# Copies, evictions and Abs on either of two engines, shorter product steps, fillers on TensorE and later stores of x in a planned retention + two-MoE kernel

## The chip, the cores and the metric

One core of a Trainium2 chip. The metric is device time in microseconds, from one launch; the kernel before has a median of 885.75 us over three runs (883.87 to 886.39).

## The reference, cut to what matters

Retention (attention without softmax, with a decay mask) over 4 batches, 8 heads, 576 positions of 64, then two dense feed-forward layers of 512 to 2048 to 512 on 2304 tokens.

```python
scores = q @ k.T / 8
x = (scores * Dmat) @ v             # Dmat[i, j] = gamma[h] ** (i - j) for i >= j, else 0
h = x @ moe_w_in
x = (h * cos(h)) @ moe_w_out
h = x @ moe2_w_in
out = (maximum(h, 0) + log1p(exp(-abs(h)))) @ moe2_w_out
```

## The kernel before, in words

**Number format.** Each fp32 operand of the two MoE layers is split in a high part (fp32r, made by a copy on ScalarE) and a low part (the difference, made by `sub`, L270, on VectorE or GpSimd). A product is three matmuls: high by high, high by low, low by high.

**A plan orders everything.** The kernel is written as some 3,500 steps (`op`): an engine, a cost in us, a key (when the step is wanted, in the plan's own clock), a function that issues the instructions, and tokens read and written. `Plan.order` runs a list schedule: of the steps whose inputs are there, the one that can start first goes next, and among equals the one with the lower key. Each engine's instruction stream is then issued in that order, and an engine works through its stream in order. A step of the kind "pool or dve" is put on GpSimd or VectorE, whichever gives the lower start + FLEX x cost. `port` keeps GpSimd and the VectorE steps marked with `port=True` apart in the plan. DMAs (`dma`, L262) all go out from SyncE's queue and never before key - LEAD (7.381) in the plan. `t_mm`, `t_act`, `t_dve`, `t_dve2`, `t_pool` are the costs. Tiles come from rings: a new tile waits for all users of the one whose place it takes.

**Attention.** 32 pieces (`piece`, L652 on: `front`, `masks`, `states`, `back`, `after`), each one pair of heads and half a sequence: fp32 scores on TensorE (L529), masks on VectorE, the state sums (L534, L584, L588), values and carried parts (L606), then the high and low part of x (L641, L270). The first 16 pieces run alone; the other 16 lie between the steps of the first MoE groups (`SPREAD`). Before the first piece three warm-up matmuls of 350 zero columns run (L900). `raw` is the tile that a piece's q, k, v load fills (ring of 5).

**Layer 1, part A** (`moe_a`, `slot`, `mm_in` L693, `out1` L789): five groups of tokens (512, 512, 384, 384, 512), the first 8 of 16 blocks of the hidden width. `x_store(m)` writes a group's x (xdh, xdl) to device memory for the rest of the layer. The partial sums are copied out of PSUM (`ev`, L935) and stored as pd. Weights come as 64-bit-viewed words and are put together from bits (`convert`: L317 and L323 on ScalarE, L329, L336 or L332, L336, L340 on VectorE; then wh, L363, and wl, L270).

**The rest** (`moe_c`, `quad`) is three phases of five token blocks by four pairs of hidden blocks: the second half of layer 1 and the two halves of layer 2. A quad of 512 tokens makes seven products of half-size blocks instead of eight (a Strassen-like scheme): product 1 into R1, 2 into R2, 5 into R3; copy_1 (L847) and copy_5 (L851) save R1 and R3; one step then does products 6 (on R1) and 3 (on R3); copy_6 (L854) saves R1; L860 adds both copies to R2 and R3; product 7 goes onto R1, L863 makes R4 from R1 and the saved R3, and product 4 ends R1. Product matmuls have the line L823, 256 columns each, six to a product. `activate` is the nonlinearity: layer 1 scales to turns (L729), takes the remainder (L733), Abs (L736), Sin (L739) and the product (L742); layer 2 uses L753, Softplus (L756) and L759. Then gh (L768, ScalarE) and gl (L270, VectorE) feed the output matmuls (L884, up to 512 columns). Results are added to what was stored (L1105) or, in the first phase of layer 2, copied out of PSUM (`ev`, L1095). While a phase runs, `weight_pair` makes the next pairs of weights (L394, L415, L423) and `x_load_c` the next block of x (L1013, L1020).

The plan's clock has marks: M[m], when group m of part A begins, and MB, when the quads begin (`M0` plus the groups' costs). Before the change M0 = 27.414.

Of the kernel before, what the change touches and what calls it, by code (L numbers as in the profile page):

```python
# [32 lines left out]
def t_mm(n, m=128):  # L33
    return max(n / 2236.0 + 0.001, 0.107 * m / 128)
# [24 lines left out]
POOL_DVE = "pool or dve"  # L59

# [6 lines left out]
FLEX = 0.364  # L67
# [33 lines left out]
class Plan:  # L101
# [29 lines left out]
    def order(self):  # L131
# [32 lines left out]
        for _ in range(n):  # L164
            best = None
            for i in can:
                eng, dur, key, _, _, uses_port, _ = self.ops[i]
                if eng == POOL_DVE:
# [10 lines left out]
            t, _, i, dur, eng = best  # L179
            can.remove(i)  # L180
# [14 lines left out]
            if uses_port or what == POOL_DVE:  # L195
                port = t + dur
# [27 lines left out]
def retention_moe_moe(ctx, tc, qkv, w1, w2, mask, mtail, dq, dk, out):  # L224
# [128 lines left out]
    def weight(layer, f, key, step):  # L353
        wk = ("w", layer, f)
        for z in range(2):
# [16 lines left out]
            op(POOL_DVE, 512, k + 2.8, lo, r=[ak, th], w=[tl])  # L372
# [284 lines left out]
    def piece(firsts, seconds, backs, K):  # L657
# [13 lines left out]
        op("pe", sum(p["dur"] for p in ps) + 0.35, K, run, r=[t for p in ps for t in p["r"]],  # L671
# [48 lines left out]
    def activate(layer, e, h_k, n, i, K1):  # L720
# [5 lines left out]
        if layer == 1:  # L726
# [8 lines left out]
            def a4():  # L735
                nc.scalar.activation(e["r"], e["r"], AF.Abs)  # L736
# [9 lines left out]
            op("act", t_act(n), K1 + 1.4, a4, r=[r_k], w=[r_k])  # L746
# [51 lines left out]
    def quad(layer, q, xk, n, K, u, acc_id, acc, first, last):  # L798
# [40 lines left out]
        if n == 512:  # L839
# [5 lines left out]
            def copy_1():  # L845
                e["cv"] = wp["q"].tile([128, 512], F32, tag="cv", name="cv", bufs=2)
                nc.scalar.activation(e["cv"][:, 0:256], R1(), AF.Copy)  # L847

            def copy_5():
                e["c5"] = wp["q"].tile([128, 256], F32, tag="c5", name="c5", bufs=2)  # L850
                nc.scalar.activation(e["c5"], R3(), AF.Copy)  # L851

            def copy_6():
                nc.scalar.activation(e["cv"][:, 256:512], R1(), AF.Copy)  # L854
# [334 lines left out]
```

## Time and profile before

| | |
|---|---|
| median of three runs | 885.75 us |
| the profiled run's own time | 888.67 us |
| its span, first to last instruction | 886.9 us |
| TensorE busy | 860.3 us (97%) |
| VectorE busy | 606.1 us (68%) |
| ScalarE busy | 488.5 us (55%) |
| GpSimd busy | 134.8 us (15%) |
| mean granted TensorE clock | 0.994 |

A matmul's busy time includes the tail of the pipeline, so neighbours overlap and the busy share does not say how near the engine is to its peak; its idle time is real. The same holds for the durations of VectorE and ScalarE: the next instruction starts a little before the end of the one before. DVE is VectorE, ACT is ScalarE, PE is TensorE and PEld its weight load, POOL is GpSimd, SPq is SyncE's queue. `L823 <- ACT cv L847` reads: line 823 waited for what ScalarE wrote to cv on line 847.

### The profile page before, as it was taken

Reading aid. Unit: us, or ns where it says so; the run is one execution under the profiler, and the core shown is the slowest. Engines: PE = TensorE matmul, PEld = TensorE weight load, DVE = VectorE, ACT = ScalarE, POOL = GpSimd, SP = SyncE. Lnnn points to the kernel's source line nnn. Section 1 sums busy time; section 2 is a strip of 40 time slices with the busy share of each in tenths; the row PEclk is TensorE's granted clock in tenths of the full one; section 3 lists DMA queues with packets and bytes.
Section 4 is the critical chain, followed back from the end, with each engine's and each line's share of the span. In section 5 each row is a group of like instructions: output and inputs, shape, how many; then the busy total and the mean of one; then the engine's idle time right before and its main releaser. Section 6 shows DMA issues by size and latency. Waiting matters only on the chain.

```text
span 886.9 us, 15054 instructions
## 1 busy us (share of the span) xinstructions
PE 860.3 (97%) x5766; PEld 748.5 (84%) x5766; DVE 606.1 (68%) x1107; ACT 488.5 (55%) x984; POOL 134.8 (15%) x143
## 2 busy tenths in 40 slices
PE   8999999999999999999999999999999999999998
PEld 5766777899988888888888888898898989898887
DVE  3799744564499986567588997467559985464554
ACT  1477743545577865546777875355547863333322
POOL 3622000100031260022053341020001010000000
PEclk8999999999999999999999999999999999999999
DMA  9886323432325612226355628065453925241202
GB/s 317 347 322 225 123 81 131 165 133 92 119 99 163 229 49 95 87 86 191 107 209 180 197 75 308 17 257 204 141 215 122 351 104 195 114 148 72 95 31 77
DMA packets 56233, 139.14 MB, mean 157 GB/s; under 512 B 5088, under 2 KB 24672, under 8 KB 54112
## 3 DMA queue, kind: packets, MB, share of 16 engines
q1 hardware_dynamic: 56160, 138.18, 44.2%
q8 instruction: 45, 0.74, 0.3%
q14 instruction: 28, 0.23, 0.1%
HBM read 93.59 MB, written 44.56 MB: 156 GB/s over the span
## 4 chain that ended last, share of the span: by engine, by line
PE 73%; DVE 9%; DMA 7%; ACT 5%; issue 3%; SPq 1%; POOL 1%; DVEq 0%; POOLq 0%; ACTq 0%
PE acc L884 26%; PE acc L789 10%; PE o L823 7%; PE hb L823 7%; PE ha L823 5%; PE s L823 5%; PE hb L693 4%; PE ha L693 3%; DMA wr<-in_w 2%; PE o L606 1%; SPq L262 1%; DVE wk L329 1%; PE s L693 1%; PE o L693 1%; DVE gl L270 1%
## 5 line engine op out<-in xcount | busy, mean ns | idle before, releaser
L884 PE MATMUL acc<-pair,gh 128*128 128x512 f32 x576 | 180.1, 393 | 0.0
L884 PE MATMUL acc<-pair,gl 128*128 128x512 f32 x288 | 113.6, 394 | 0.0
L884 PEld LDWEIGHTS acc<-pair,gh 128*128 128x128 f32 x576 | 99.4, 188 | 14.9 <-ACT gh L768 0.4
L884 PE MATMUL acc<-gh,pair 128*128 128x512 f32 (+1 forms) x320 | 103.4, 375 | 2.2 <-DVE pt L1105 1.4
L756 ACT ACTIVATE er<-er 128x512 f32<-128x512 f32 (+1 forms) x80 | 47.1, 589 | 76.3 <-DVE er L753 76.2
L823 PE MATMUL o<-x,pair 128*128 128x256 f32 x328 | 78.0, 282 | 2.5 <-ACT cv L847 2.3
L823 PE MATMUL o<-xx,pair 128*128 128x256 f32 x320 | 77.5, 284 | 2.0 <-DVE o L863 1.4
L823 PE MATMUL hb<-x,pair 128*128 128x256 f32 x328 | 77.9, 281 | 1.4 <-DVE hb L863 0.8
L823 PE MATMUL hb<-xx,pair 128*128 128x256 f32 x320 | 77.0, 282 | 1.0 <-DVE hb L863 1.0
L884 PEld LDWEIGHTS acc<-gh,pair 128*128 128x128 f32 x320 | 59.5, 192 | 11.2 <-DVE pt L1105 1.6
L884 PEld LDWEIGHTS acc<-pair,gl 128*128 128x128 f32 x288 | 54.0, 188 | 13.2 <-DVE gl L270 0.5
L884 PE MATMUL acc<-gl,pair 128*128 128x512 f32 (+1 forms) x160 | 60.8, 380 | 3.5 <-DVE gl L270 3.5
L736 ACT ACTIVATE er<-er 128x512 f32<-128x512 f32 (+2 forms) x80 | 46.9, 586 | 31.3 <-DVE er L733 30.1
L823 PEld LDWEIGHTS o<-x,pair 128*128 128x128 f32 x328 | 57.6, 188 | 7.6 <-ACT cv L847 2.9
L823 PEld LDWEIGHTS hb<-x,pair 128*128 128x128 f32 x328 | 57.6, 188 | 6.6 <-DVE hb L863 1.5
L823 PEld LDWEIGHTS o<-xx,pair 128*128 128x128 f32 x320 | 56.3, 188 | 7.6 <-DVE o L863 3.1
L823 PEld LDWEIGHTS hb<-xx,pair 128*128 128x128 f32 x320 | 56.3, 188 | 5.8 <-DVE hb L863 2.0
L789 PE MATMUL acc<-gh,wh 128*128 128x512 f32 (+1 forms) x160 | 60.2, 376 | 0.5 <-ACT gh L768 0.5
L789 PE MATMUL acc<-gl,wh 128*128 128x512 f32 (+1 forms) x160 | 59.4, 372 | 0.8 <-DVE gl L270 0.7
L789 PE MATMUL acc<-gh,wl 128*128 128x512 f32 (+1 forms) x160 | 58.9, 368 | 0.0
L823 PE MATMUL s<-x,pair 128*128 128x256 f32 x256 | 58.3, 280 | 0.0
L823 PE MATMUL ha<-x,pair 128*128 128x256 f32 x256 | 58.2, 279 | 0.0
(197 smaller groups left out, 2073.2 us busy)
## 6 DMA issues: line engine op xcount, KB each, us to landing
wr<-in_w SPq DMA_DIRECT2D x64, 512.0 KB, 4.0
raw<-in_qkv SPq DMA_DIRECT2D x12, 640.0 KB, 7.2
raw<-in_qkv SPq DMA_DIRECT2D x12, 512.0 KB, 5.7
od<-pt SPq DMA_DIRECT2D x18, 256.0 KB, 3.9
pt<-od SPq DMA_DIRECT2D x18, 256.0 KB, 2.8
out<-pt SPq DMA_DIRECT2D x18, 256.0 KB, 2.1
pt<-pd SPq DMA_DIRECT2D x16, 256.0 KB, 3.1
yd<-pt SPq DMA_DIRECT2D x16, 256.0 KB, 2.1
```

The lines of the kernel that those rows point to most:

```text
L262: nc.sync.dma_start(dst(), src())
L270: e.tensor_tensor(out_, a, hi.bitcast(F32), ALU.subtract)
L329: nc.vector.scalar_tensor_tensor(T["wk", u], T["wy", u], 3, T["wr", u][:, :, 0], ALU.logical_shift_left, ALU.bitwise_or)
L606: nc.tensor.matmul(o_at(z)[Z[j]], lhs(j), rhs(j), start=start, stop=stop, skip_group_check=True)
L693: nc.tensor.matmul(h_[:, 0:n], lhs, rhs[:, d, 0:n], start=(k == 0), stop=(k == 3 * NC - 1))
L736: nc.scalar.activation(e["r"], e["r"], AF.Abs)
L756: nc.scalar.activation(e["r"], e["r"], AF.Softplus)
L789: nc.tensor.matmul(acc[o][:, 0:n], l[:, s], e[r], start=(first and z == 0), stop=(last and z == 2))
L823: nc.tensor.matmul(out_, w_(a), x_(b), start=(start and y == 0), stop=(stop and y == 5), skip_group_check=True)
L884: nc.tensor.matmul(acc[m][:, 0:n] if layer == 1 else acc[m], l, r, start=(begin and z == 0), stop=(stop and z == 2))
```

## The change

Five things: (1) a new kind of step, "act or dve", for the three copies of a quad, the two kinds of eviction (`ev`) and Abs of layer 1 (on VectorE Abs is a bitwise and with 0x7FFFFFFF); (2) products 6 and 3 become two steps with keys of their own, and copies and adds of a quad get keys EARLY or EARLY_2 lower; (3) after pieces 0 and 1 two and five matmuls of 128 zero columns; (4) x_store's key goes from M + 30 to M + 60; (5) other constants of the plan. AHEAD is empty, so its loop in `order` does nothing, and LO_A keeps its step as it was.

```diff
-def t_mm(n, m=128):
-    return max(n / 2236.0 + 0.001, 0.107 * m / 128)
+def t_mm(n):
+    return n / 2236.0 + (0.0035 if n == 256 else 0.001)
...
+ACT_DVE = "act or dve"
...
-FLEX = 0.364
+FLEX = 0.27
+FLEX_AD = 0.824
...
-W2 = (16.989, 6.589, 8.458, 3.942)
-W3 = (16.475, 1.639)
-XC = 4.126
-LAG_C = 1.17
+W2 = (18.111, 6.589, 14.31, 1.214)
+W3 = (16.671, 1.958)
+XC = 3.809
+LAG_C = 1.049
 TT = 3
+TURN = 0.6
+XS = 60.0
+FILL = (2, 5)
+EARLY = 12.734
+EARLY_2 = 8.236
...
-LL = 1.121
+LL = 0.916
...
-W0 = (34.558, 4.019, 3.451)
-M0 = 27.414
+W0 = (39.65, 2.003, 3.451)
+M0 = 28.787
 AK = (1.0, 2.2)
-PAIR_A = 0.566
+PAIR_A = 0.959
...
+                elif eng == ACT_DVE:
+                    t, d, e = min(
+                        ((max(ready[i], free[e], port if e == "dve" and uses_port else 0.0), d, e) for e, d in zip(("act", "dve"), dur)),
+                        key=lambda o: o[0] + FLEX_AD * o[1])
...
-            if uses_port or what == POOL_DVE:
+            if uses_port and eng != "act" or what == POOL_DVE:
                 port = t + dur
...
+    def copy(eng, out_, in_):
+        if eng is nc.scalar:
+            nc.scalar.activation(out_, in_, AF.Copy)
+        else:
+            eng.tensor_copy(out_, in_)
...
-        op("pe", sum(p["dur"] for p in ps) + 0.35, K, run, r=[t for p in ps for t in p["r"]],
+        op("pe", sum(p["dur"] for p in ps) + TURN, K, run, r=[t for p in ps for t in p["r"]],
...
-            dma(lambda g=g: xd[g][:, :, r0:r0 + n], lambda g=g: T[xk][g][:, :, 0:n].bitcast(F32), 512 * n * 4, M[m] + 30 + g, r=XT[m], w=[("xd", g, m)])
+            dma(lambda g=g: xd[g][:, :, r0:r0 + n], lambda g=g: T[xk][g][:, :, 0:n].bitcast(F32), 512 * n * 4, M[m] + XS + g, r=XT[m], w=[("xd", g, m)])
...
-            def a4():
-                nc.scalar.activation(e["r"], e["r"], AF.Abs)
+            def a4(eng):
+                if eng is nc.scalar:
+                    nc.scalar.activation(e["r"], e["r"], AF.Abs)
+                else:
+                    r = e["r"].bitcast(I32)
+                    nc.vector.tensor_scalar(r, r, 0x7FFFFFFF, None, ALU.bitwise_and)
...
-            op("act", t_act(n), K1 + 1.4, a4, r=[r_k], w=[r_k])
+            op(ACT_DVE, (t_act(n), t_dve2(n)), K1 + 1.4, a4, r=[r_k], w=[r_k], port=True)
...
-            op("act", t_act(256, True), K + 0.7, copy_1, r=[r1, ("qopen",)], w=[(ck, 0)], new=[("cv", 2, ck)])
-            op("act", t_act(256, True), K + 2.1, copy_5, r=[r3, ("qopen",)], w=[(c5k,)], new=[("c5", 2, c5k)])
-            pe([P(R1, 6, False), P(R3, 3, False)], K + 1.0, [r1, r3])
-            op("act", t_act(256, True), K + 4.0, copy_6, r=[r1], w=[(ck, 1)])
-            op("dve", t_dve(512), K + 4.5, lambda: nc.vector.tensor_tensor(ea["h"], ea["h"], e["cv"], ALU.add),
+            op(ACT_DVE, (t_act(256, True), t_dve(256)), K + 0.7 - EARLY, copy_1, r=[r1, ("qopen",)], w=[(ck, 0)], new=[("cv", 2, ck)])
+            op(ACT_DVE, (t_act(256, True), t_dve(256)), K + 2.1 - EARLY, copy_5, r=[r3, ("qopen",)], w=[(c5k,)], new=[("c5", 2, c5k)])
+            pe([P(R1, 6, False)], K + 0.9, [r1])
+            pe([P(R3, 3, False)], K + 1.5, [r3])
+            op(ACT_DVE, (t_act(256, True), t_dve(256)), K + 4.0 - EARLY, copy_6, r=[r1], w=[(ck, 1)])
+            op("dve", t_dve(512), K + 4.5 - EARLY_2, lambda: nc.vector.tensor_tensor(ea["h"], ea["h"], e["cv"], ALU.add),
                r=[(ck, 0), (ck, 1)], w=[r2, r3])
             pe([P(R1, 7, False)], K + 2.0, [r1])
-            op("dve", t_dve(256), K + 5.5, lambda: nc.vector.tensor_tensor(R4(), R1(), e["c5"], ALU.add), r=[r1, (c5k,)], w=[r4])
+            op("dve", t_dve(256), K + 5.5 - EARLY, lambda: nc.vector.tensor_tensor(R4(), R1(), e["c5"], ALU.add), r=[r1, (c5k,)], w=[r4])
...
+    def fill(n, times):
+        for _ in range(times):
+            nc.tensor.matmul(T["warm", "o"][:, 0:n], T["warm"][:, 0:128], T["warm"][:, 0:n], start=True, stop=True)
...
-            op("act", t_act(n, True), K, ev, r=[(ak,)], w=[pk], new=[("pt", PT, pk[0])])
+            op(ACT_DVE, (t_act(n, True), t_dve(n)), K, ev, r=[(ak,)], w=[pk], new=[("pt", PT, pk[0])])
...
+        if i < len(FILL) and FILL[i]:
+            op("pe", FILL[i] * t_mm32(128), AK[0] + AK[1] * i + 0.1, lambda i=i: fill(128, FILL[i]), r=[U[i]["x"][0], (("er", "warm"),)],
+               w=[(("hb", "warm"),)])
...
-                op("act", t_act(DM, True), K, ev, r=[(ak,)], w=[(pk,)], new=[("pt", PT, pk)])
+                op(ACT_DVE, (t_act(DM, True), t_dve(DM)), K, ev, r=[(ak,)], w=[(pk,)], new=[("pt", PT, pk)])
```

## Rows read from the trace of the kernel before

**Rows 1.** Busy us by stretch; each engine's (x instructions), then PEclk, DMA share, GB/s.

```profile
0.00:9.00 9.00, 5.75 (x30) 3.35 (x30) 1.30 (x4) 1.51 (x2) 2.24 (x9) 1.00 0.74 229
9.00:15.82 6.82, 6.28 (x60) 4.87 (x60) 2.96 (x9) 1.06 (x4) 2.85 (x6) 0.50 1.02 355
15.82:45.00 29.18, 28.55 (x488) 22.17 (x488) 22.12 (x79) 10.79 (x33) 16.91 (x26) 1.00 0.92 360
45.00:100.00 55.00, 50.14 (x350) 38.10 (x346) 50.85 (x99) 41.30 (x82) 10.79 (x14) 1.00 0.75 260
...
281.00:345.00 64.00, 59.88 (x369) 52.11 (x368) 56.30 (x92) 46.83 (x91) 21.01 (x16) 1.00 0.45 149
345.00:380.00 35.00, 35.00 (x212) 30.74 (x211) 18.96 (x32) 19.50 (x38) 1.73 (x2) 1.00 0.24 76
380.00:420.00 40.00, 36.62 (x268) 34.06 (x267) 28.21 (x54) 21.12 (x49) 8.39 (x6) 0.96 0.43 136
...
440.00:532.00 92.00, 88.06 (x540) 76.78 (x540) 80.24 (x125) 70.58 (x139) 36.04 (x33) 1.00 0.48 161
...
600.00:620.00 20.00, 18.36 (x120) 16.21 (x119) 15.61 (x26) 11.45 (x24) 1.68 (x1) 1.00 0.53 204
620.00:886.90 266.90, 262.68 (x1632) 234.78 (x1630) 168.65 (x284) 118.32 (x236) 9.50 (x12) 1.00 0.38 140
sum 886.90, PE 860.30 PEld 748.55 DVE 606.13 ACT 488.54 POOL 134.83; mean PE 66.18 PEld 57.58 DVE 46.63 ACT 37.58 POOL 10.37
```

**Rows 2.** Waits of TensorE: line and what it waited for, total us, times, longest.

```profile
PE acc L884 <- DVE gl L270: 3.5, 7, 1.4
PE o L823 <- ACT cv L847: 2.9, 3, 1.3
...
PE ha L693 <- ACT wh L363: 1.9, 1, 1.9
PE s L529 <- DVE st L588: 1.8, 1, 1.8
PE hb L823 <- DVE hb L863: 1.8, 2, 1.0
...
PE o L823 <- DVE o L863: 1.4, 1, 1.4
```

**Rows 3.** Busy us in the second half-clock stretch, columns as in rows 1.

```profile
391.29:394.70 3.41, 3.41 (x14) 3.18 (x15) 1.18 (x4) 1.18 (x4) 0.00 (x0) 0.50 0.15 43
```

**Rows 4.** TensorE in order of time, start: us, start, duration, [idle before <- releaser].

```profile
1.45 3.87 PE L900 MATMUL hb<-er 128*128 128x350 f32 x6 [1.45 <-DVE er L895]
...
6.83 0.71 PE L529 MATMUL acc<-raw 64*128 64x128 f32 x8 [0.73 <-DMA raw<-in_qkv]
...
9.54 1.23 PE L529 MATMUL acc<-raw 64*128 64x128 f32 x8 [1.61 <-DMA raw<-in_qkv]
...
18.17 0.72 PE L529 MATMUL acc<-raw 64*128 64x128 f32 x8
```

**Rows 5.** SyncE's queue in order of time, the first store of x.

```profile
55.03 0.58 SPq L262 DMA_DIRECT2D xdh<-x  x1
```

**Rows 6.** ScalarE in order of time, before the wait for wh.

```profile
73.58 0.67 ACT L323 ACTIVATE wr<-wr 128x512 int32<-128x512 uint8 x1 [2.14 <-DMA wr<-in_w]
```

**Rows 7.** ScalarE in order of time, ahead of a late copy_1.

```profile
454.88 0.63 ACT L736 ACTIVATE er<-er 128x512 f32<-128x512 f32 x1 [1.24 <-DVE er L733]
455.42 0.62 ACT L1020 ACTIVATE xx<-tt 128x512 fp32r<-128x512 f32 x1
...
457.03 0.37 ACT L847 ACTIVATE cv<-o 128x256 f32<-128x256 f32 x1
```

**Rows 8.** VectorE in order of time, the two adds of a quad.

```profile
530.06 0.69 DVE L860 TENSOR_TENSOR s<-s,cv 128x512 f32<-128x512 f32 x1
530.66 0.42 DVE L863 TENSOR_TENSOR o<-o,c 128x256 f32<-128x256 f32 x1
```

**Rows 9.** Line 332: duration in ns (min/median/max), first and last start in us, forms.

```profile
L332 DVE TENSOR_SCALAR wk<-wy x16: 413/420/1506, 180.6 to 317.4; 128x512 int32<-128x512 int32 x16
```

More of the change, by code (lines that the diff above doesn't have):

```diff
@@ L74 @@
 WB = (21.627, 3.294)
-W2 = (16.989, 6.589, 8.458, 3.942)
-W3 = (16.475, 1.639)
-XC = 4.126
-LAG_C = 1.17
+W2 = (18.111, 6.589, 14.31, 1.214)
+W3 = (16.671, 1.958)
+XC = 3.809
+LAG_C = 1.049
 TT = 3
+TURN = 0.6
[3 more added lines that the diff above has]
+EARLY_2 = 8.236
+AHEAD = {}
+GAP = 2.0
+LO_A = "pool or dve"
 END = 3.1
 LC = 2.5
-LL = 1.121
+LL = 0.916
 LB = 1.9
@@ L179, in order @@
             t, _, i, dur, eng = best
+            if eng in AHEAD and dur > AHEAD[eng]:
+                for j in can:
+                    e, d, key = self.ops[j][:3]
+                    if j != i and e == eng and key < self.ops[i][2] - GAP and ready[j] < t + AHEAD[eng]:
+                        f = max(free[eng], ready[j], port if self.ops[j][5] else 0.0)
+                        if f < t + AHEAD[eng] and (f, key) < (t + AHEAD[eng], best[1]):
+                            best, t, i, dur = (f, key), f, j, d
             can.remove(i)
@@ L214, in emit @@
     def emit(self, nc):
-        flexible = {"pool": nc.gpsimd, "dve": nc.vector}
+        flexible = {"pool": nc.gpsimd, "dve": nc.vector, "act": nc.scalar}
         for i in self.order():
-            if self.ops[i][0] == POOL_DVE:
+            if self.ops[i][0] in (POOL_DVE, ACT_DVE):
                 self.ops[i][3](flexible[self.eng[i]])
@@ L371, in weight @@
                new=[(f"w{f}", 1, wk)] if z == 0 else [])
-            op(POOL_DVE, 512, k + 2.8, lo, r=[ak, th], w=[tl])
+            if LO_A == POOL_DVE:
+                op(POOL_DVE, 512, k + 2.8, lo, r=[ak, th], w=[tl])
+            else:
+                op("pool", t_pool(512), k + 2.8, lambda lo=lo: lo(nc.gpsimd), r=[ak, th], w=[tl], port=True)
     def weight_pair(layer, q, key, step):
@@ L843, in quad, with copy_1, copy_5, copy_6 @@
             e = {}
[L845 removed]
+            def copy_1(eng):
                 e["cv"] = wp["q"].tile([128, 512], F32, tag="cv", name="cv", bufs=2)
[L847 to L849 removed]
+                copy(eng, e["cv"][:, 0:256], R1())
+            def copy_5(eng):
                 e["c5"] = wp["q"].tile([128, 256], F32, tag="c5", name="c5", bufs=2)
[L851 to L860 removed]
+                copy(eng, e["c5"], R3())
+            def copy_6(eng):
+                copy(eng, e["cv"][:, 256:512], R1())
+            op(ACT_DVE, (t_act(256, True), t_dve(256)), K + 0.7 - EARLY, copy_1, r=[r1, ("qopen",)], w=[(ck, 0)], new=[("cv", 2, ck)])
[4 more added lines that the diff above has]
+            op("dve", t_dve(512), K + 4.5 - EARLY_2, lambda: nc.vector.tensor_tensor(ea["h"], ea["h"], e["cv"], ALU.add),
                r=[(ck, 0), (ck, 1)], w=[r2, r3])
             pe([P(R1, 7, False)], K + 2.0, [r1])
[L863 removed]
+            op("dve", t_dve(256), K + 5.5 - EARLY, lambda: nc.vector.tensor_tensor(R4(), R1(), e["c5"], ALU.add), r=[r1, (c5k,)], w=[r4])
             pe([P(R1, 4, False)], K + 3.0, [r1])
@@ L897, in warm @@
     def warm():
-        o_ = bank("hb")
-        for _ in range(3):
-            nc.tensor.matmul(o_[:, 0:WARM], T["warm"][:, 0:128], T["warm"][:, 0:WARM], start=True, stop=True)
+        T["warm", "o"] = bank("hb")
+        fill(WARM, 3)
+    def fill(n, times):
+        for _ in range(times):
+            nc.tensor.matmul(T["warm", "o"][:, 0:n], T["warm"][:, 0:128], T["warm"][:, 0:n], start=True, stop=True)
     if WARM:
```

9 lines of the change are left out of this document (5 added, 4 removed).

## The prediction

> **What bounds the kernel now.** I read the table of stretches first [rows 1]. TensorE is busy 860.30 of 886.90 us, so only 26.6 us are idle, and the table says where: 3.25 us before 9.00, 0.54 and 0.63 in the next two stretches, 4.86 from 45 to 100, 4.12 from 281 to 345, 3.38 from 380 to 420, 3.94 from 440 to 532, 1.64 from 600 to 620, 4.22 after 620 (nearly all the drain of the last store). The long stretches left out have 0.02. So this is a TensorE kernel with holes. The reader should see what the holes have in common: from 281 to 345 VectorE is busy 56.30 of 64 us (88%), from 440 to 532 80.24 of 92 (87%), and ScalarE 73% and 77%; from 345 to 380 VectorE is at 54% and TensorE loses nothing. The holes sit where weight conversion crowds the two elementwise engines.
>
> Second, TensorE's waits [rows 2]. The product steps (L823) wait 2.9 us for the copy L847 and 1.8 and 1.4 us for the add L863: 6.1 us in six waits. The output steps (L884) wait 3.5 us for gl (L270). In the first 100 us there are a 1.8 us wait for st and a 1.9 us wait for wh.
>
> Third, the clock. From 9.00 to 15.82 it is granted at 0.50, which is 1.2 GHz [rows 1], and again from 391.29 to 394.70 [rows 3].
>
> **The change, part by part.**
>
> *Fillers.* Two zero matmuls follow piece 0, five follow piece 1. Before the clock falls, TensorE stands 0.73 us ahead of piece 1 and 1.61 ahead of piece 2, both times for a load of raw; the eight score matmuls of a piece then take 1.23 us at half clock and 0.72 at full clock [rows 4]. The nearest price of a filler is the warm-up: six records, three matmuls of 350 columns, 3.87 us, so at most 0.47 us for 128 columns, and half of that at full clock. Seven cost 1.6 to 3.3 us against 2.34 us of standing; at the price nearest to theirs (the clock is full there) they fit, at the other end up to 1 us spills over. What they can give: 6.28 busy us at half clock hold 3.1 us of work that full clock would not need. But in that stretch the DMA engines are 1.02 busy at 355 GB/s and stay at 0.92 until 45, so faster pieces soon run into their loads. I take 2.0 us, from -1 to 3.1. The Trainium skill (TensorE: Matmul & The Clock Gate, Terms) puts the loss at throttled time times (1 - K/N); for both half-clock stretches together that is 5.1 us as an estimate, where busy time gives 4.8 and the loads, which that rule leaves out, leave less.
>
> *Later stores of x.* x_store moves from M+30 to M+60 in key: five pairs of issues on SP's queue move behind weight and qkv loads. The first pair is issued at 55.03 [rows 5], among the loads for the first MoE slots, when the DMA engines are 0.75 busy; ScalarE then stands 2.14 us for a weight load before L323 [rows 6], and the weight behind it ends in the 1.9 us wait for wh. W0's new keys (step 2.003 for 4.019) also bring later weights forward. Of the 4.86 us from 45 to 100 I take 2.5, from 0 to 4.9. What the move holds up: the store of group 2 frees the pool of the pair weights. By the constants M[2]+60-7.4 is 179 and the first pair's key M[3]+18.1 is 184, against the start of the quads at MB = 244, so this hides. The store of group 4 falls at M[4]+60-7.4 = 252, after MB, and tile x1 that it holds is wanted by the quads of the second block, whose turn is four quads of UC, 42 us, after MB. That hides too.
>
> *Copies of the quads (copy_1, copy_5, copy_6) and their adds.* They get keys 12.7 (the 512-wide add 8.2) earlier and may go to either engine. See one case: copy_1 stood in ScalarE's queue behind L736, L1020 and more, none of which the product step was waiting for; it waited until it ran at 457.03 [rows 7]. On VectorE the add L863 stood behind L860 from 530.06 to 530.66 and TensorE waited for it [rows 8]. With an early key a copy that is ready goes next, so what remains of a wait is the rest of the instruction in work, about 0.3 us (half of 0.6). Six waits of 6.1 us become 1.8: I take 4.5, from 0 to 6.1. On VectorE a copy from PSUM should cost about what L863 does, 0.42 us, against 0.37 for L847 on ScalarE [rows 7, 8]: either engine will do.
>
> *Shorter product steps.* Products 6 and 3 become two steps, so copy_6 may start after six matmuls instead of twelve and product 3 fills TensorE meanwhile. It adds no instruction. It pays in the few small waits on L854, below the rows shown, so I take 0.5, from 0 to 1.
>
> *Abs and evictions on either engine.* Abs costs 0.63 us on ScalarE [rows 7]. The nearest row on VectorE, a one-source integer operation of the same tile, has a median of 0.42 and a longest of 1.51 [rows 9]. This, with the copies leaving ScalarE's queue, shortens the chain to gl; but the copies now also jump ahead of gl on VectorE. Of gl's 3.5 us I take 2, from -3 to 3.5.
>
> *Clock at 391.* Half clock over 3.41 us costs 1.7; it follows TensorE's waits there. With shorter waits it may not fall: 1.0, from 0 to 1.7.
>
> *VectorE's extra load.* Whatever moves to it in the crowded stretches delays conversion: minus 1, from 0 to minus 4.4 (second rival). *The other constants* (t_mm, TURN, FLEX, M0, LL and the rest) only shift keys and the planner's clock. They add no instruction; what they reorder is hidden by the quiet stretches [rows 1], and where it isn't, it belongs to the terms above.
>
> Sum: 2.0 + 2.5 + 4.5 + 0.5 + 2 + 1 - 1 = 11.5 us. The profiled run took 888.67 us for a span of 886.9, 2.9 above the median of 885.75; I subtract from the median: 885.75 - 11.5 = 874.25, say **874.3**. With all upper ends (20.3) it would be 865.5; with the lower ends (-8.4) 894.
>
> **Rivals.** *The waits change hands.* The order on each engine is fixed in advance, so a copy that goes first makes gl or gh late: copies gain 4.5, gl loses 3, Abs and clock give nothing, start and x stores give 1: 885.75 - 2.5 = 883.2. For it: gl is already the longest wait [rows 2]. Against: a late copy holds up a whole quad, a late gl only one output group, behind which products can run.
>
> *VectorE becomes the bound.* In the three crowded stretches from 281 to 532 (196 us) VectorE has 31.3 us free [rows 1]. About 18 quads of 10.9 us pass in them (an estimate: a quad's 66 matmuls at the pace of 345 to 380, 212 in 35 us); three copies and two Abs on VectorE at 0.42 us less some 0.07 of overlap between neighbours (L863 starts 0.60 us after an L860 of 0.69) bring 5 x 0.35 = 1.75 us to each, 31.5 us in all, and fill it. From 54% to 88% busy the idle share of TensorE rose from 0 to 6.4%; on the same slope the last 12% cost 2.3% of 196 us, 4.4 us, and the gains of copies and gl go. 885.75 - 2 (start) + 4.4 = 888.2. It decides if more than about two thirds of the moved operations land on VectorE there. Against: the planner takes whichever engine starts and ends first, and ScalarE is the freer one. A rule of the Trainium skill speaks for this rival: GPSIMD Engine Reference, Specifications, says that GpSimd shares its SBUF interfaces with VectorE and contends with instructions in a two-port mode, which Abs on VectorE would be; rows 9 agree, with 1.51 us for what mostly takes 0.42.
>
> *The plan hardly uses it.* ScalarE stays first choice, the order stays nearly as it was, and only the start gains: 885.75 - 1.5 = 884.3.
>
> **How the numbers follow.** Forecast 0.69 (its own range 866 to 882), waits change hands 0.12, VectorE the bound 0.13, hardly used 0.06. About 0.3% (2.7 us, so 883.1) is what a measurement of this kernel can tell from no change. Faster: 0.69 and half of 0.12, 0.75. Same: the other half and the 0.06, 0.12. Slower: 0.13. The range is 864 to 887: it takes in the upper ends, both rivals near no change, and leaves out about 0.04 below and 0.11 above.
>
> **What would show it.** Fillers: granted clock 1.00 from 9 to 16, and the first MoE matmul about 2 us earlier. Stores: xdh first issued after 75, and no 1.9 us wait for wh. Copies: L823's waits for L847 and L863 sum to under 2 us. Abs: L736 on both engines. If VectorE goes over 93% busy in 281 to 345 and TensorE idles more there than 4.12 us, the second rival is right. If gl's waits pass 6 us, the first is. The prediction is wrong if the first 100 us or the quads keep their idle time.

## The result: 0.8% slower

The changed kernel has a median of **892.77 us** over five runs (891.21 to 895.03) beside 885.75 us for the kernel before (883.87 to 888.51) on the same chip: a ratio of 1.0082, interval 1.0055 to 1.011. The forecast of 874.3 us was wrong in its sign. The profiled runs lie closer together (892.48 against 888.67 us, spans 890.7 and 886.9), since the profile of before comes from a run 2.9 us above its median, and that of after from one 0.3 below. The changed kernel's busy times:

```profile
PE 861.9 (97%) x5780; PEld 751.2 (84%) x5780; DVE 633.0 (71%) x1169; ACT 454.2 (51%) x897; POOL 170.2 (19%) x168
```

Before it was 606.1 us and 1107 instructions on VectorE, 488.5 and 984 on ScalarE, 134.8 and 143 on GpSimd. ScalarE lost 87 instructions: the copies, evictions and Abs that went to VectorE. VectorE has only 62 more, because **25 of its own went to GpSimd**. The diff has no line that says so; it is what the plan did with the new constants and the new kind of step. The 25 lie all over the kernel: 6 more from 281 to 345, 5 from 100 to 281, none from 440 to 532 (33 in both kernels), 7 behind 620.

The stretches of the changed kernel, columns as in [rows 1]:

```profile
9.00:15.82 6.82, 6.31 (x96) 4.69 (x95) 3.66 (x12) 1.44 (x5) 2.95 (x7) 1.00 1.05 365
...
281.00:345.00 64.00, 60.39 (x374) 54.09 (x372) 58.72 (x97) 44.56 (x84) 27.38 (x23) 0.97 0.45 152
...
440.00:532.00 92.00, 83.62 (x511) 73.39 (x511) 84.82 (x130) 64.97 (x123) 37.66 (x33) 0.99 0.45 152
```

The fillers did what they say: 9.00 to 15.82 runs at full clock. But from 440 to 532 TensorE is idle for 8.38 us where it was 3.94, with VectorE at 92%. And the clock fell elsewhere, three times, as its own stretches show:

```profile
49.07:52.48 3.41, 3.41 (x24) 2.55 (x24) 2.07 (x8) 2.04 (x6) 1.28 (x1) 0.50 1.02 400
318.72:322.13 3.41, 3.41 (x16) 3.41 (x17) 2.84 (x6) 2.03 (x4) 1.27 (x2) 0.50 0.00 0
530.35:533.76 3.41, 2.87 (x10) 2.59 (x11) 3.27 (x7) 0.88 (x2) 0.00 (x0) 0.50 0.10 11
```

Each follows or overlaps a stop of TensorE (2.65, 2.74 and 3.16 us). That makes 10.23 us at 0.50, as much as before (6.82 in [rows 1] and 3.41 in [rows 3]): in these two executions the half clock moved, it did not shrink. Over all its runs the changed kernel was granted 0.993 on the mean, the kernel before between 0.995 and 0.996 in the runs beside which the experiments were timed; as an estimate (the difference times 890 us), 2 to 3 of the 7.0 us between the medians go with the clock, which fell where TensorE stood. The waits of TensorE name the stops (L857 is the product step, L823 before; L919 the output step; L295 and L297 are copies on ScalarE and VectorE; L898 is the add L863 of before):

```profile
PE o L857 <- ACT cv L295: 3.9, 4, 2.7
PE o L857 <- DVE o L898: 3.8, 2, 3.2
PE s L559 <- ACT x L671: 2.6, 1, 2.6
PE acc L919 <- DVE gl L291: 2.3, 4, 1.6
PE hb L857 <- DVE hb L898: 1.9, 1, 1.9
...
PE o L857 <- DVE cv L297: 1.5, 2, 0.9
...
PE hb L857 <- ACT cv L295: 1.2, 1, 1.2
...
PE hb L857 <- DVE cv L297: 0.9, 1, 0.9
```

The product steps' waits for copies and adds sum to 13.2 us. Before, the rows of the same kind sum to 7.4: 6.1 in [rows 2], and 1.3 in four more:

```profile
PE s L823 <- ACT c L851: 0.4, 1, 0.4
PE hb L823 <- ACT cv L854: 0.3, 1, 0.3
PE hb L823 <- ACT cv L847: 0.3, 1, 0.3
PE o L823 <- ACT cv L854: 0.3, 1, 0.3
```

Of the 3.5 us that the output steps of the quads waited for gl 2.3 are left.

Where in time it went (each edge is a phase's first matmul): from the first MoE matmul (49.90 before, 51.18 after) and on to the quads (281.48, 280.86) and to layer 2 (488.15, 482.92) the changed kernel came out 5.2 us ahead. It lost 5.7 us in one block, the first of layer 2, and 3.4 behind it. The lead of 5.2 us hangs on the run of before that was profiled: b_fill_fixed and b_store_fixed below, with its order, reach layer 2 at 485.26 and 484.41. The block's length does not: 50.52 us in both of these, and 56.03 in a_swap, with the order of the changed kernel. That block, in the kernel before and in the changed one:

```profile
488.15:538.71 50.56, 48.33 (x284) 40.98 (x282) 47.73 (x77) 39.95 (x77) 21.04 (x20) 1.00 0.41 132
```

```profile
482.92:539.16 56.24, 49.74 (x286) 42.83 (x285) 54.04 (x84) 39.32 (x74) 20.85 (x19) 0.97 0.39 126
```

TensorE's idle time went from 2.23 to 6.50 us, its busy time up by 1.4 (the half clock). VectorE has 6.3 us more, with seven instructions more. GpSimd has no more to do here than before (19 instructions for 20). What makes the block so long is seen in the order of time, VectorE first, then GpSimd, then TensorE, of the changed kernel:

```profile
523.99 1.78 DVE L291 TENSOR_TENSOR pair<-wk,pair 128x512 fp32r<-128x512 f32 x1
525.69 1.78 DVE L363 SCALAR_TENSOR_TENSOR wk<-wy,wk 128x512 int32<-128x512 int32 x1
527.39 0.69 DVE L895 TENSOR_TENSOR s<-s,cv 128x512 f32<-128x512 f32 x1
528.11 0.69 DVE L787 TENSOR_SCALAR er<-s 128x512 int32<-128x512 int32 x1
528.72 1.77 DVE L291 TENSOR_TENSOR pair<-wk,pair 128x512 fp32r<-128x512 f32 x1
530.41 0.42 DVE L898 TENSOR_TENSOR o<-o,c 128x256 f32<-128x256 f32 x1
```

```profile
522.22 1.29 POOL L1054 TENSOR_TENSOR tt<-xx,tt 128x512 f32<-128x512 f32 x1 [0.63 <-DVE pair L291]
523.47 1.75 POOL L291 TENSOR_TENSOR xx<-xx,x 128x512 fp32r<-128x512 f32 x1
525.18 1.74 POOL L291 TENSOR_TENSOR xx<-tt,x 128x512 fp32r<-128x512 f32 x1
527.00 1.60 POOL L1054 TENSOR_TENSOR tt<-xx,tt 128x512 f32<-128x512 f32 x1
528.67 1.27 POOL L291 TENSOR_TENSOR xx<-xx,x 128x512 fp32r<-128x512 f32 x1
```

```profile
530.89 0.58 PE L857 MATMUL o<-xx,pair 128*128 128x256 f32 x1 [3.16 <-DVE o L898]
```

Line 363 has a median of 0.683 us over its 64 instructions and a longest of 1.776. Beside GpSimd's steps three VectorE instructions take 1.78 us; L895 and L787, whose s is in PSUM, keep to 0.69. The add that TensorE waits for stands behind all of them in VectorE's queue. So in this block it is not more work for GpSimd but the place of the work: the new order sets these conversions and GpSimd's chain side by side, ahead of the add.

The stop of 2.74 us at 318 comes by the same road, over ScalarE. A copy stands in its queue behind L453, which waits for L367 of VectorE, and L367 takes 1.77 us beside GpSimd (one row each of VectorE and GpSimd, two of ScalarE, one of TensorE):

```profile
315.01 1.77 DVE L367 SCALAR_TENSOR_TENSOR wk<-wr,wk 128x512 int32<-128x512 int32 x1
...
314.62 1.61 POOL L1054 TENSOR_TENSOR tt<-tt 128x512 f32<-128x512 f32 x1
...
316.81 0.63 ACT L453 ACTIVATE pair<-wk 128x512 fp32r<-128x512 f32 x1 [2.74 <-DVE wk L367]
...
318.25 0.38 ACT L295 ACTIVATE cv<-o 128x256 f32<-128x256 f32 x1
...
318.68 0.58 PE L857 MATMUL o<-x,pair 128*128 128x256 f32 x1 [2.74 <-ACT cv L295]
```

The third stop, 2.65 us in the attention, was not followed.

### The profile page after: what moved, and what is told of

It reads as the page before. It is cut to its first block, busy times and chain, and to the rows that moved or that the text cites. A ratio compares the mean times of both kernels' runs of the same rounds, so it can differ in the third digit from the quotient of the medians.

```text
span 890.7 us, 15157 instructions
## 1 busy us (share of the span) xinstructions
PE 861.9 (97%) x5780; PEld 751.2 (84%) x5780; DVE 633.0 (71%) x1169; ACT 454.2 (51%) x897; POOL 170.2 (19%) x168
## 4 chain that ended last, share of the span: by engine, by line
PE 75%; DVE 11%; DMA 5%; ACT 4%; issue 3%; SPq 1%; POOL 0%; DVEq 0%; POOLq 0%; ACTq 0%
PE acc L919 27%; PE acc L823 9%; PE o L857 8%; PE hb L857 7%; PE s L857 6%; PE ha L857 5%; PE ha L723 4%; PE hb L723 3%; PE o L636 2%; DMA wr<-in_w 2%; DVE wk L363 2%; DMA pt<-pd 1%; DVE pair L291 1%; PE s L559 1%; DVE wk L356 1%
## 5 line engine op out<-in xcount | busy, mean ns | idle before, releaser
L919 PE MATMUL acc<-pair,gh 128*128 128x512 f32 x576 | 180.8, 395 | 0.1
L919 PE MATMUL acc<-pair,gl 128*128 128x512 f32 x288 | 114.0, 396 | 2.1 <-DVE gl L291 2.1
L919 PEld LDWEIGHTS acc<-pair,gh 128*128 128x128 f32 x576 | 101.0, 189 | 16.5 <-ACT gh L802 0.6
L919 PE MATMUL acc<-gh,pair 128*128 128x512 f32 (+1 forms) x320 | 100.2, 370 | 0.3 <-ACT gh L802 0.3
L857 PE MATMUL o<-xx,pair 128*128 128x256 f32 x320 | 79.4, 290 | 6.2 <-DVE o L898 3.8
L857 PE MATMUL o<-x,pair 128*128 128x256 f32 x328 | 79.8, 287 | 3.1 <-ACT cv L295 3.1
L857 PE MATMUL hb<-x,pair 128*128 128x256 f32 x328 | 78.6, 283 | 3.9 <-DVE hb L898 1.9
L857 PE MATMUL hb<-xx,pair 128*128 128x256 f32 x320 | 78.0, 286 | 0.1
L857 PEld LDWEIGHTS o<-xx,pair 128*128 128x128 f32 x320 | 57.4, 191 | 12.9 <-DVE o L898 7.1
L919 PEld LDWEIGHTS acc<-pair,gl 128*128 128x128 f32 x288 | 54.2, 188 | 16.0 <-DVE gl L291 3.4
L773 ACT ACTIVATE er<-er,hp_t 128x512 f32<-128x512 f32 (+2 forms) x80 | 54.1, 679 | 24.0 <-DVE er L770 23.1
L919 PEld LDWEIGHTS acc<-gh,pair 128*128 128x128 f32 x320 | 58.5, 188 | 9.1 <-ACT gh L802 0.5
L857 PEld LDWEIGHTS o<-x,pair 128*128 128x128 f32 x328 | 58.8, 192 | 7.8 <-ACT cv L295 4.1
L857 PEld LDWEIGHTS hb<-x,pair 128*128 128x128 f32 x328 | 57.6, 188 | 8.9 <-DVE hb L898 3.4
L823 PE MATMUL acc<-gh,wh 128*128 128x512 f32 (+1 forms) x160 | 60.4, 377 | 0.3 <-ACT gh L802 0.3
L857 PEld LDWEIGHTS hb<-xx,pair 128*128 128x128 f32 x320 | 56.4, 188 | 4.9 <-DVE hb L898 2.4
L823 PE MATMUL acc<-gl,wh 128*128 128x512 f32 (+1 forms) x160 | 59.2, 370 | 1.3 <-DVE gl L291 1.2
L919 PE MATMUL acc<-gl,pair 128*128 128x512 f32 (+1 forms) x160 | 59.3, 370 | 0.2 <-DVE gl L291 0.2
L823 PE MATMUL acc<-gh,wl 128*128 128x512 f32 (+1 forms) x160 | 58.9, 368 | 0.0
L857 PE MATMUL s<-x,pair 128*128 128x256 f32 x256 | 58.8, 282 | 0.0
L857 PE MATMUL ha<-x,pair 128*128 128x256 f32 x256 | 58.3, 280 | 0.0
```

What stands on the lines that cost most here:

```text
L773: nc.scalar.activation(e["r"], e["r"], AF.Sin, bias=hp_t[:, 0:1], scale=-1.0)
L823: nc.tensor.matmul(acc[o][:, 0:n], l[:, s], e[r], start=(first and z == 0), stop=(last and z == 2))
L857: nc.tensor.matmul(out_, w_(a), x_(b), start=(start and y == 0), stop=(stop and y == 5), skip_group_check=True)
L919: nc.tensor.matmul(acc[m][:, 0:n] if layer == 1 else acc[m], l, r, start=(begin and z == 0), stop=(stop and z == 2))
```

## The experiments

**A measure.** "VectorE's lost time" below is worked out from each trace: for every VectorE instruction its duration less the shortest of its form, summed where that is over 0.06 us. It is 39.5 us before and 51.6 after. Some 17 to 20 us of it, in every kernel, are only differences between lines of one form: taken within each line it is 21.9 and 31.9 us. All VectorE instructions of over 1 us, 23 before and 33 after, overlap one of GpSimd's.

**1. GpSimd's reads taken out of either kernel** (a_thin on after, b_thin on before; Thin stands for nc.gpsimd where a planned step is issued, so the order of each kernel is kept):

```diff
+class Thin:
+    def tensor_tensor(self, out, x, y, op):
+        if len(out.shape) != 2 or out.shape[-1] < 256:
+            self.e.tensor_tensor(out, x, y, op)
+            return
+        self.e.memset(out.bitcast(F32), 0.0)
+        self.e.tensor_tensor(out[:, 0:32], x[:, 0:32], y[:, 0:32], op)
```

> The changed kernel with every engine's order kept, but each 256- or 512-column difference or sum that the plan gives GpSimd is cut to 32 columns, and a memset of zero fills the rest (this part of the computation is left out). Crowding theory (two-input VectorE instructions are slowed from 0.68 to 1.78 us beside GpSimd's, and the change gives GpSimd 25 more): the VectorE instructions over 1 us go, TensorE's waits for L898 and L295 in the stretches 281 to 345 and 440 to 540 fall by half, and the time falls from 892.8 to 884 or less. Rival (VectorE's additional copies and Abs are the cost): VectorE still carries them, the time stays within 3 us of 892.8. Rival (shorter steps, early keys): it stays as well.

> The kernel before with the same cut of GpSimd's steps (the same part of the computation left out). Crowding theory: here GpSimd has less, so it gains less, 3 to 6 us (to about 881), and the changed kernel with the cut comes out level with or below this one. Rivals: both move by the same small amount, and the changed one stays 5 us or more above.

Measured: a_thin 877.78 us (ratio to before 0.9915, 0.9883 to 0.9946), 15.0 below the changed kernel; b_thin 873.73 us (0.9874, 0.9852 to 0.9895), 12.0 below the kernel before. The lost time within each line falls to 2.4 and 1.5 us. So GpSimd's wide two-input steps cost both kernels more than any other thing tried, and the changed one by 3.0 us more. With them out, the changed kernel is still 4.0 us behind: what those are stays open.

**2. Single parts, planned anew.** On after: copies, evictions and Abs only on ScalarE (a_act); products 6 and 3 in one step again (a_merged); the same with stores at M + 30 (am_xs30); fewer steps for GpSimd (a_flex100). On before: fillers (b_fill), two product steps (b_split), stores at M + 60 (b_xs60), early keys (b_early).

```diff
# a_act, in Plan.order
-for e, d in zip(("act", "dve"), dur)
+for e, d in zip(("act",), dur)
# a_merged; b_split is the reverse on the kernel before
-pe([P(R1, 6, False)], K + 0.9, [r1])
-pe([P(R3, 3, False)], K + 1.5, [r3])
+pe([P(R1, 6, False), P(R3, 3, False)], K + 1.0, [r1, r3])
# am_xs30: that, and
-XS = 60.0
+XS = 30.0
# a_flex100
-FLEX = 0.27
+FLEX = 1.0
```

> The changed kernel, but the plan must put every copy, eviction and Abs on ScalarE, as before; all else is kept, and the order is planned anew. VectorE theory: VectorE loses some 70 instructions, 27 us of work, and the time falls to 887 or less. Crowding theory: GpSimd keeps 113 of its 131 flexible steps, so the time stays between 888 and 895.

> The changed kernel with products 6 and 3 in one step again; the order is planned anew. Short-step theory (product 7 follows product 3 at once and finds copy_6 not ready): the quiet last phase gains back 1.5 to 2 us and the whole 3 to 5, to about 888. Crowding theory: 130 flexible steps stay on GpSimd, so it stays within 3 us of 892.8.

> The changed kernel with two parts undone: products 6 and 3 in one step, and the stores of x at M + 30. If each part's cost is its own (5.4 us for the steps, 8.5 for the stores, as alone), it is clear of both, at 880 or less. If the parts' costs are mostly those of a new plan, it lies where the others lie, 885 to 892.

> The changed kernel with FLEX at 1.0 for 0.27, so that the plan gives GpSimd 73 flexible steps for 131. Crowding theory: the time that VectorE's instructions lose falls from 51.6 us by a third or more, and, if that outweighs the work that VectorE takes over, the time falls to 886 or less. If VectorE's own load is what bounds (rival), it takes over some 40 us of work and the time rises to 895 or more.

> The kernel before with only the fillers added (two and five matmuls of 128 zero columns after pieces 0 and 1), planned anew. My prediction's term: the clock stays full from 9 to 16 and the time falls by 2 us, to about 883.5. Load theory (the pieces then run into their loads of raw): the clock stays full, but the first MoE matmul is no earlier than 49.5 and the time stays within 1 us of 885.5.

> The kernel before with only products 6 and 3 made two steps with the keys of the change, planned anew. My prediction's term: 0 to 1 us faster. Short-step theory (product 7 then follows product 3 without outputs between them and waits for copy_6, and product 4 for L863): the last phase from its second block on is 1.5 to 2 us longer and the whole 3 to 5 us slower, about 889.

> The kernel before with only the stores of x moved to M + 60, planned anew. My prediction's term: 2.5 us faster, with the second MoE group starting 2 us or more ahead of 104.4. Rival: the stores are no part of the loss before 100, group 1 starts within 1 us of 104.4, and the time stays within 2 us of 885.5.

> The kernel before with only the keys of the quads' copies and adds lowered by 12.734 and 8.236, all copies still on ScalarE, planned anew. My prediction's term: TensorE's waits of L823 for L847 and L863 fall from 6.1 us to 2 or less and the time falls by 4.5, to about 881. Rival (the order is already fixed by when a copy's input is ready, and late VectorE work is what delays it): the waits stay above 4 us and the time is not below 885.

Measured, with the ratio to the kernel before: a_act 889.19 (1.0046, 1.0025 to 1.0068), a_merged 888.21 (1.0042, 1.0022 to 1.0063), am_xs30 893.18 (1.0079, 1.0048 to 1.0109), a_flex100 899.3 (1.0164, 1.0132 to 1.0195), b_fill 888.15 (1.0029, 1.0009 to 1.005), b_split 890.65 (1.0056, 1.0037 to 1.0075), b_xs60 893.73 (1.0101, 1.0071 to 1.013), b_early 891.35 (1.0067, 1.0043 to 1.0092). All are slower than before, even those with one small edit. Of the 8.0 us by which the span of b_xs60 exceeds that of before, 1.9 are there when the quads begin, 4.9 come between there and 545, long after the first stores, and 1.3 behind that. Since each new key makes the plan order everything anew, two controls followed, in which one constant moves by 3% or less and no part of the change is made:

```diff
# b_xc425
-XC = 4.126
+XC = 4.25
# b_r219
-R0 = 22.0
+R0 = 21.9
```

> A control: the kernel before with one constant of the plan moved a little (XC 4.25 for 4.126: the next block of x is wanted 0.124 us earlier). No step, engine kind or cost changes; some 110 of TensorE's steps and 240 of ScalarE's change places. If the orders of neighbouring plans are worth the same on the chip, it stays within 1 us of 885.3. If a new plan by itself costs (the order of before is a lucky one among its neighbours), it is 3 to 8 us slower, as the kernels with one part of the change are.

> A second control: the kernel before with R0 at 21.9 for 22.0 (loads of q, k, v wanted 0.1 us later); 66 of TensorE's steps and 168 of ScalarE's change places. The two answers as for the first control: within 1 us of 885.3, or 3 to 8 us slower.

Measured: 888.93 (1.0035, 1.0018 to 1.0052) and 888.73 (1.0034, 1.0017 to 1.0051). **Two neutral new plans cost about 3 us each**: the order of before is better than these two neighbours. Of the eight kernels, then, b_fill, a_merged, a_act and b_split can't be told from a mere new plan; the others came out worse than both controls, but two controls don't show how far a new plan can stray. a_flex100 has a likely cause of its own: its GpSimd is busy for 94.5 us only, but VectorE for 652.2, and it is the slowest of all. Fewer steps on GpSimd were no cure where VectorE had to take them; with the order kept this was not tested.

**3. Parts with the order of the steps kept.** b_fill_fixed issues the fillers inside pieces 0 and 1; b_store_fixed moves the first pair of stores to 84.51 us, just ahead of the second pair; a_swap issues product 4 behind the next output step in 44 of 48 quads; a_thin25 is a_thin with every third 512-column step only.

```diff
# b_fill_fixed, at the end of a piece's step
+if firsts in ([0], [1]):
+    fill(128, (2, 5)[firsts[0]])
# b_store_fixed, in emit; late[m] are the stores of group m
+for i in self.late[0]:
+    order.remove(i)
+at = order.index(self.late[1][0])
+order[at:at] = self.late[0]
# a_swap, in emit; fours are the steps of product 4
+for i in self.fours:
+    at = order.index(i)
+    to = next(k for k in range(at + 1, len(order)) if self.eng[order[k]] == "pe")
+    if self.ops[order[to]][3].__name__ == "mo" and self.start[order[to]] - self.end[i] < 0.15:
+        order.insert(to, order.pop(at))
# a_thin25, in Thin (written shorter)
-if len(out.shape) != 2 or out.shape[-1] < 256:
+self.n += len(out.shape) == 2 and out.shape[-1] >= 512
+if len(out.shape) != 2 or out.shape[-1] < 512 or self.n % 3:
```

> The kernel before with its order kept on every engine and the two and five fillers put in behind pieces 0 and 1. My prediction's term: the clock stays full from 9 to 16 and the time falls by 2 us, to 883.5. Load theory: the pieces run into their loads, the first MoE matmul is less than 1 us earlier, and the time stays within 1 us of 885.5.

> The kernel before with its order kept, but the first two stores of x (issued at 55.03 and 55.67) go out with the next two, at about 87. My prediction's term: weight loads land earlier, the 1.9 us wait for wh goes, the second MoE group starts 2 us earlier and the time falls by 2.5, to 883. Rival: nothing waits for these loads, the time stays within 1 us of 885.5.

> The changed kernel with its order kept on every engine, but in 44 of its 48 quads product 4 changes places with the output step after it, so that the add L898 has 0.69 us more. Short-step theory: the 12 weight-load waits for L898 (3.2 us) from 735 to 855 go, and the time falls by 3 to 5 us, to 888 to 890. If the shorter steps cost only by planning anew: within 1 us of 892.8.

> The changed kernel with its order kept, but 25 of GpSimd's 512-column steps (every third) are cut to 32 columns, with a memset of zero for the rest (that part of the computation is left out): as many as the change gave it. Crowding theory: VectorE's lost time falls from 51.6 us to about 40, as before the change, and the time falls by 3 us or more, to 890 or less. Otherwise: within 1.5 us of 892.8.

*b_fill_fixed*: 886.62 us (1.0005, 0.9991 to 1.0019). Its second and third stretch, against those of [rows 1]:

```profile
9.00:15.82 6.82, 6.24 (x94) 4.78 (x95) 3.88 (x12) 1.44 (x5) 2.93 (x6) 1.00 1.05 354
15.82:45.00 29.18, 26.73 (x432) 20.80 (x428) 19.30 (x69) 8.53 (x29) 15.64 (x24) 0.94 0.89 338
```

Full clock up to 15.82 and 94 matmuls in place of 60, but the clock falls behind that, at 21.36 for 3.41 us, and the first MoE matmul comes at 51.77, not earlier than the 49.90 of before (this mark differs by 2.7 us between the profiles of the changed kernel and of a_swap, whose starts are the same). TensorE's wait for raw from GpSimd went from 0.6 to 2.4 us. Over its 12 runs the granted clock is 0.9965 on the mean, beside 0.9958 in the 29 of before: the fillers moved the half clock and hardly shortened it. What a start without any half clock would be worth is therefore not tested.

*b_store_fixed*: 885.23 us (0.9991, 0.9976 to 1.0005). The wait for wh is gone and group 1 begins at 101.85, 2.5 us earlier than the 104.40 of before; nothing of it arrives at the end.

*a_swap*: 893.94 us (1.0084, 1.0069 to 1.0099). Its twelve weight loads from 735 to 855 no longer wait for L898, as they do in the changed kernel; no gain. Product 4's place is not the cause.

*a_thin25*: **884.43 us** (0.9985, 0.9973 to 0.9996), 8.3 below the changed kernel, with VectorE's lost time at 39.8 us. With as many of GpSimd's wide steps thinned as it had got more, the changed kernel is as fast as before. Of the 25, three are in the first block of layer 2, which had got none. But its thinned steps also end 0.5 to 0.9 us earlier, so GpSimd's lateness was still a rival.

**4. Reads or lateness; and GpSimd's work alone.** a_long25 is a_thin25 with the memset issued twice. b_pool_extra is the kernel before, in its own order, with additions nobody reads.

```diff
# a_long25
 self.e.memset(out.bitcast(F32), 0.0)
+self.e.memset(out.bitcast(F32), 0.0)
# b_pool_extra, behind every fourth planned step of GpSimd; scr is 128x256
+for _ in range(2):
+    nc.gpsimd.tensor_tensor(scr, scr, scr, ALU.add)
```

> The changed kernel with its order kept; the same 25 of GpSimd's 512-column steps as in the run that thinned every third read 32 columns only, but now two memsets of the whole tile come before each, so that a step takes as long as before: 0.53 + 0.53 + 0.33 = 1.39 us, where the full steps of the thinned run average 1.41 (the tile's other columns are zero, so these 25 steps' results are left out). If what hurts is that VectorE's two-input instructions are stretched while GpSimd reads its two inputs, the gain of the thinned run stays: 883 to 886 us, VectorE's lost time near 40 us. If what hurts is that GpSimd is a slow engine that hands its results on late, the gain goes: 891 to 894 us. A memset that itself slows VectorE would give values between.

> The kernel before with its order kept; ahead of every fourth of GpSimd's planned steps two additions of 128x256 on a scratch tile that nobody reads, some 44 to 52 instructions of about 0.78 us, that is as many columns as 22 to 26 steps of 512. If crowding by GpSimd is the cause, this kernel alone should lose what the change lost, as far as the additions fall beside VectorE's two-input work: 889 to 895 us, with VectorE's lost time up from 39.5 us to 46 or more. If the loss came from the new plan's order and not from GpSimd's extra work, 885 to 887.5 us.

*a_long25*: 886.06 us (1.0000, 0.9989 to 1.0012), GpSimd busy for 165.9 us (170.2 in the changed kernel), lost time 41.1. So 6.7 of the 8.3 us stay gained without GpSimd being faster: what the thinning takes away **is the reads**. The other 1.6 are GpSimd's time, the memsets or the scatter of the runs. The same steps as shown above, on VectorE, GpSimd and TensorE (GpSimd's step from 525.18 above is here two memsets and a short addition):

```profile
520.72 1.78 DVE L308 TENSOR_TENSOR pair<-wk,pair 128x512 fp32r<-128x512 f32 x1
522.42 0.68 DVE L380 SCALAR_TENSOR_TENSOR wk<-wy,wk 128x512 int32<-128x512 int32 x1
...
524.35 0.89 DVE L308 TENSOR_TENSOR pair<-wk,pair 128x512 fp32r<-128x512 f32 x1
525.16 0.42 DVE L915 TENSOR_TENSOR o<-o,c 128x256 f32<-128x256 f32 x1
```

```profile
520.20 1.75 POOL L254 TENSOR_TENSOR xx<-xx,x 128x512 fp32r<-128x512 f32 x1
521.89 0.52 POOL L256 MEMSET xx<- 128x512 f32 x1
522.47 0.53 POOL L257 MEMSET xx<- 128x512 f32 x1
523.08 0.25 POOL L258 TENSOR_TENSOR xx<-tt,x 128x32 fp32r<-128x32 f32 x1
```

```profile
525.64 0.39 PE L874 MATMUL o<-xx,pair 128*128 128x256 f32 x1 [1.21 <-DVE o L915]
```

Beside a memset L380 (L363 above) takes 0.68 us, not 1.78. From the first pair to the add it is 4.44 us, not 6.42, and TensorE stops for 1.21, not 3.16. The block of layer 2 takes 51.96 us here.

*b_pool_extra*: **892.26 us** (1.0067, 1.0051 to 1.0083), lost time 45.6. It had 52 such additions, 39.8 us of them, and no other edit. Its first block of layer 2, and there VectorE, GpSimd and TensorE:

```profile
484.75:540.30 55.55, 49.79 (x283) 40.66 (x282) 50.79 (x75) 39.36 (x76) 29.26 (x31) 1.00 0.37 115
```

```profile
528.34 1.10 DVE L272 TENSOR_TENSOR pair<-wk,pair 128x512 fp32r<-128x512 f32 x1
529.36 1.77 DVE L338 SCALAR_TENSOR_TENSOR wk<-wy,wk 128x512 int32<-128x512 int32 x1
...
532.26 0.42 DVE L865 TENSOR_TENSOR o<-o,c 128x256 f32<-128x256 f32 x1
```

```profile
526.62 2.26 POOL L1133 TENSOR_TENSOR scr<-scr 128x256 f32<-128x256 f32 x2
528.85 1.73 POOL L272 TENSOR_TENSOR xx<-xx,x 128x512 fp32r<-128x512 f32 x1
```

```profile
532.73 0.39 PE L825 MATMUL o<-xx,pair 128*128 128x256 f32 x1 [2.37 <-DVE o L865]
```

The additions alone bring the same loss, most of it in the same block (55.55 us against 50.56), before the same add. Here the clock stays at 1.00, so the loss does not need the clock. The additions also make GpSimd's own steps later; this run does not part the two, a_long25 does.

All kernels that keep an order, by lost time:

| order of | kernel | GpSimd busy us | VectorE's lost us | median us |
|---|---|---|---|---|
| before | b_thin | 93.0 | 18.9 | 873.73 |
| after | a_thin | 111.7 | 21.8 | 877.78 |
| before | before | 134.8 | 39.5 | 885.75 |
| before | b_fill_fixed | 134.3 | 39.5 | 886.62 |
| before | b_store_fixed | 135.1 | 39.8 | 885.23 |
| after | a_thin25 | 154.2 | 39.8 | 884.43 |
| after | a_long25 | 165.9 | 41.1 | 886.06 |
| before | b_pool_extra | 174.7 | 45.6 | 892.26 |
| after | a_swap | 170.8 | 50.1 | 893.94 |
| after | after | 170.2 | 51.6 | 892.77 |

The lost time goes roughly with the median, whichever order it is. Among the kernels planned anew it does so less well: b_xs60 (40.1) and a_flex100 (39.5) are slow for reasons that the lost time does not show.

No version beat the kernel before by more than its measurement tells, with the whole result computed.

## Why the prediction was wrong

**The step that failed** is the price of nothing for a new order of steps. The prediction says of the other constants that they "only shift keys and the planner's clock", "add no instruction", and that what they reorder "is hidden by the quiet stretches"; and of an early copy or add that only "the rest of the instruction in work, about 0.3 us" remains of its wait. No term of the sum holds that VectorE's two-input steps are slow beside GpSimd's. The runs showed in its place that the new order and the new division of the work set more of them side by side: instructions of 1.78 us for 0.68, a block of 56.24 us for 50.56, and 13.2 us of waits for 7.4. I costed this at nothing; taking 25 reads out of the changed order gives 6.7 us back (a_long25), and adding reads to the order of before costs 6.5 (b_pool_extra).

**What remains open is how much of the 7.0 us this is, and what brought it.** With all wide reads out of both kernels the changed one still lies 4.0 us behind, so by that difference the reads are 3.0; two neutral new plans cost about 3 us each. Between 3.0 and 6.7 us is as far as the runs go. The number of GpSimd's two-input steps rose from 138 to 163 (145 to 163 in the kernels planned with FLEX at 0.27, 131 to 138 with 0.364, 105 with 1.0), since the plan decides by start + FLEX x cost. But FLEX is not all of it: a_act has every new constant and only 145, so in these plans the greater part of the 25 came with the copies, evictions and Abs that VectorE got. FLEX alone was not run. And the block that lost most had got none of the 25.

**The second rival had the place and the sign, not the road.** VectorE bounds the crowded stretches, and 888.2 us was nearer than the forecast. Its mark, 93% from 281 to 345, was not reached (92%, with TensorE idle for 3.61 us); the loss came in the later crowded stretch. But I priced 0.42 us copies and Abs. The 26.9 us that VectorE is busier include 12.1 of lost time (51.6 less 39.5; 10.0 within each line). I had the sign of it in hand: L332's 1.51 us beside a median of 0.42 [rows 9], which overlaps a GpSimd step. The trace of before also has an L329 of 1.78 us beside GpSimd at 470.55, a row that I did not use. The rule I cited there for Abs also speaks of two SBUF inputs (the Trainium skill, GPSIMD Engine Reference, Specifications); it should have been applied to every SBUF addition. A sharper form of it (the Trainium skill, SBUF — State Buffer, section "SBUF: two separate sides") says the shared pair of ports is locked for a whole instruction and the other engine waits. The trace agrees, with VectorE ending 0.55 us after GpSimd twice in a row, as the last section shows.

**Term by term.**
- *Fillers and start, 2.0*: the clock rose from 9 to 15.82 as said, the time didn't: b_fill_fixed 1.0005. The half clock came back at 21.36, and GpSimd's raw was late next; my caveat named only the loads.
- *Stores, 2.5*: the first goes out at 82.32 and the wait for wh is gone, as said; right in size where they are (2.5 in b_store_fixed, 3.7 with the rest of the change), zero at the end. I took a gain at 100 us for a gain at 886 us.
- *Copies and adds, 4.5*: wrong sign. The waits of 7.4 us (the six of 6.1 that I counted among them) became 13.2 us. I let "the rest of the instruction in work" be 0.3 us; here that instruction can be one of 1.78, and others may be queued behind it.
- *Shorter product steps, 0.5*: not resolved; a_merged is 4.6 us faster than the changed kernel, b_split slower than before, and beside some 3 us for a new plan alone neither settles it.
- *Abs and evictions, gl, 2*: gl's wait fell by 1.2 us in the quads and rose by 0.5 in part A (L789 before, L823 after). Right in direction. a_act, which takes the moves back, is no slower.
- *Clock at 391, 1.0*: that fall is gone and others came. It is no mark of the order: the profiled runs of b_fill_fixed, b_store_fixed and b_pool_extra keep the order of before and have no fall there.
- *VectorE's extra load, 1*: it was to hold the above, and was too small.

The rival that waits change hands was wrong in its place: gl did not get late, the copies and adds did.

## What to carry to other kernels

Before moving elementwise work between engines, sort the instructions by their SBUF inputs: VectorE work with two SBUF inputs and GpSimd work that reads SBUF hold each other up, and the price is read from the longest durations of a line, not from its median or the busy share. In a planned kernel compare how many steps each engine got and which of them lie side by side, and run a neutral change of a constant, before crediting an edit with a few us; then test the edit with the order kept. A gain that a milestone shows is not yet a gain at the end.

## What the runs showed of the hardware

**The hold is a whole instruction long, and goes both ways.** In the changed kernel's rows above, GpSimd's step from 523.47 ends at 525.22; VectorE's from 523.99 ends 0.55 us later, at 525.77. GpSimd's next ends at 526.92, VectorE's next at 527.47: 0.55 again. Alone the one takes 1.27 to 1.30 us and the other 0.68; taking turns, 1.75 and 1.78. Which instructions are held is seen in the groups of line 291, in the changed kernel, where gl has an input in PSUM and x has both in SBUF (after the first bar: busy us, mean ns of one):

```profile
L291 DVE TENSOR_TENSOR gl<-hb,gh 128x512 fp32r<-128x512 f32 x34 | 23.3, 685 | 12.1 <-ACT gh L802 11.8
...
L291 DVE TENSOR_TENSOR x<-x,xx 128x512 fp32r<-128x512 f32 x6 | 7.8, 1344 | 0.0
```

Of the 160 steps for gl 15 begin while a GpSimd step runs, and none takes more than 0.69 us.

**A memset on GpSimd does not hold VectorE**: 0.53 us for 128x512 in a_long25, and L380 at 0.68 beside one of them. In a_thin, with 118 memsets, 3 VectorE instructions of over 1 us are left of the 33.

**The granted clock and the time can come apart.** One of the ten executions of b_r219 was granted 0.95 in every stretch from 15.82 on, where the others had 0.988 to 0.998 on the mean; it took 888.32 us beside a median of 888.73 over all ten. Why is open.
